# One attention-plus-MoE kernel, one core: another written order ahead of the second chunk, and other places for every temporary

## The chip, the cores and the metric

The kernel runs on one core of one Trainium2 chip. The core has five engines that each work through a list of instructions of their own: TensorE (PE in the profile, its weight loads PEld), VectorE (DVE), ScalarE (ACT), GpSimd (POOL) and SyncE (SP), which here does nothing but issue transfers. The metric is the device time of one execution in microseconds (us).

## The reference

Two steps. The first is attention with 8 batches, 8 heads, 512 local and 32 global positions, head size 64. The local queries see the 32 global keys and the local keys within a window of 32, the global queries see everything:

```
s_ll = where(|i - j| <= 32, scale * q_l k_l^T, -1e9)
a_l  = softmax(concat(scale * q_l k_g^T, s_ll))
out_l = a_l @ concat(v_g, v_l)
out_g = softmax(scale * q_g k_all^T) @ v_all
```

The result is laid out as 4608 tokens of 512 values, and goes through a gated feed-forward layer of width 1536:

```
xn  = x / sqrt(mean(x*x) + 1e-6) * rms_g
g   = xn @ w_gate;  val = xn @ w_val
out = (g * sigmoid(g) * val) @ w_out
```

## The kernel before

**Tiling.** The tokens are worked in nine chunks: eight of 512 local tokens (one batch each) and a last one of the 256 global tokens. Each chunk needs its attention first, then the norm, the first layer (gate and value) and the second layer. Products in the feed-forward layers are made of f16 halves, a high and a low one of every f32 operand, with three matmuls for one. The first chunk's weights come from the inputs; while it and the second chunk run, sums of weights are formed ("folds", function fold at L1487) and stored in DRAM buffers (wa, wb, wd), and the later chunks load those.

**Pieces and their written order.** The whole program is first recorded as small pieces with a name "chunk:step.number"; one piece holds calls of one engine (write, L2076). In the first chunk L loads queries and keys, S makes scores, M takes minima on DVE, E the exponentials on ACT, T and C turn and copy them, V and A are the values, N are the steps of the root, D the factors of the norm, U (on PE) turns and scales an activation block, H and Y split it into a high and a low half, W, m, s, l, k and g prepare weights, I are the 48 pieces of the first layer and O the 24 of the second. "1:P3" is the fourth product of the second chunk, "1:S/0+2" the scores of unit 0 of the chunk after next made beside it, with N and M its minima, "1:n55" steps of the next chunk's norm, "1:w51" a step of a weight fold or load. The table ORDER (L66) lists all 3754 names, and the last loop issues them exactly so:

```
for name in ORDER.split() or list(plan):
    for call in plan.pop(name):
        call()
```

No scheduler moves anything after that: every engine, the transfer queue of SP too, executes its calls in this order and stops at the first that has to wait.

**Places.** Temporaries in the on-chip memory lie in 43 pages of 4 KB and 8 wide pages of 4.5 KB per partition; the table PAGES (L396) gives the place of each temporary in the order in which they are created ("36a" is page 36 from its first quarter on, "w3" wide page 3). The table BANKS (L444) does the same for the 8 accumulator banks of PE. Whoever writes a page or a bank waits until all earlier readers and writers of that part of it are done, engines and transfers alike. SP's transfers go round over eight lanes, and a transfer waits for the one before it on its lane.

**The places that the prediction speaks of.** The fold of the eleventh weight block ends in the piece 1:w51, whose store (L1513 to L1518) reads the original weight page with two transfers and the sums with a third. In the same stretch DVE takes the minima of the scores of 1:S/0+2 (softmax in local_halves, L969), each of which writes a scratch tile of exponentials, and PE makes a small matmul 1:n55.0 of the norm, which writes a bank that these minima read.

Of the kernel before, what the change touches and what calls it, by code (L numbers as in the profile page):

```python
# [20 lines left out]
B, H, SL, SG, D = 8, 8, 512, 32, 64  # L21
# [45 lines left out]
0:L0.0 0:S0.0 0:L2.0 0:S2.0 0:M0.0.2 0:M0.0.0 0:M0.0.1 0:z0.0 0:M0.0.3 0:M0.1.0 0:E0.0.0 0:M2.1.0  # L67
0:M2.1.1 0:M2.1.2 0:M2.1.3 0:M0.1.2 0:L3.0 0:M2.0.2 0:E2.1.0 0:M0.1.1 0:M0.1.3 0:S3.0 0:M3.1.2
0:z1.0 0:z2.0 0:M2.0.1 0:E0.1.0 0:M2.0.3 0:M2.0.0 0:E2.0.0 0:M3.0.3 0:M3.0.2 0:z2.1 0:M3.1.1
0:M3.1.0 0:M3.1.3 0:E3.1.0 0:T0.0.0 0:C0.0.0 0:L1.0 0:M3.0.1 0:M3.0.0 0:E3.0.0 0:W1.0 0:V0.0 0:z2.4  # L70
0:W0.0 0:m1.0 0:T0.1.0 0:T2.0.0 0:W3.0 0:z2.6 0:z2.5 0:l1.0 0:C2.0.0 0:m1.1 0:T2.1.0 0:C0.1.0 0:s1.0
0:l1.1 0:g1.0 0:g1.1 0:q1.0 0:z3.0 0:z4.1 0:T3.1.0 0:z4.0 0:R0.0 0:S1.0 0:M1.0.3 0:M1.0.1 0:M1.0.0
0:M1.0.2 0:V2.0 0:M1.1.1 0:M1.1.0 0:C2.1.0 0:M1.1.2 0:E1.0.0 0:M1.1.3 0:z4.2 0:R2.0 0:z2.2 0:m0.0
0:m0.1 0:s0.0 0:A0.0 0:l0.0 0:m3.0 0:E1.1.0 0:g0.0 0:m3.1 0:k3.0 0:l0.1 0:T1.1.0 0:V1.0 0:T1.0.0
0:p1.0 0:A2.0 0:s3.0 0:X0.0 0:g3.0 0:C1.0.0 0:Q0.0 0:g0.1 0:q0.0 0:T3.0.0 0:C1.1.0 0:g3.1 0:V3.0
0:X2.0 0:z2.3 0:p0.0 0:e0.0 0:e0.1 0:e0.2 0:z5.0 0:C3.0.0 0:Q2.0 0:z6.0 0:W2.0 0:C3.1.0 0:e1.0
0:q3.0 0:R3.0 0:A1.0 0:R1.0 0:Z0.0 0:e1.1 0:z6.1 0:W4.0 0:Z2.0 0:z6.2 0:X1.0 0:A3.0 0:a0.0 0:X3.0
# [2258 lines left out]
```

## Time and profile before

| | |
|---|---|
| times of three runs | 890.65, 890.77, 891.91 us, median 890.77 |
| profiled execution, first to last instruction | 890.5 us, 0.27 us under that median |
| mean granted clock of PE | 0.990 of full speed |
| busy: PE, DVE, ACT, POOL | 864.1, 709.7, 557.9, 277.8 us |
| the transfer queue's share of 16 engines | 70.9% |

In the profile one line of the source, L2095, issues everything, so instructions are told apart by operation, shape and time. "Idle" behind a row is the idle time of the engine ahead of it, and the name behind the arrow is what ended it. The part of the order that the change rearranges ends in this execution at about 168.6 us, when the scores 1:S/0+1 are done.

### The profile page before, as it was taken

What the parts mean: (1) busy time and instruction counts of PE and PEld (TensorE: products, weight loads), DVE (VectorE), ACT (ScalarE), POOL (GpSimd) and SP (SyncE); (2) the same over time, 40 slices, a digit from 0 to 9 for tenths busy, and PEclk for the clock granted to TensorE, in tenths of its full rate; (3) what the DMA queues carried; (4) which work ended last, traced back from release to release, by engine and by line L of the source; (5) the groups of instructions that cost most, each with busy time, mean ns of one, the idle gap of its engine ahead of it and who ended that gap; (6) DMA issues with size and microseconds to landing.
All of it is one profiled execution on the core that took longest, in us unless ns stands there. A gap on an engine that the chain in (4) does not pass through costs nothing.

```text
span 890.5 us, 28310 instructions
## 1 busy us (share of the span) xinstructions
PE 864.1 (97%) x11646; PEld 666.4 (75%) x11646; DVE 709.7 (80%) x1857; ACT 557.9 (63%) x1362; POOL 277.8 (31%) x255
## 2 busy tenths in 40 slices
PE   5599999999999999999999999999999999999998
PEld 4554455545548885588888888888888888888997
DVE  5999999798686776777886899688886798587576
ACT  6999993657344664557473876568575772545343
POOL 0000000024834475414531255123441344124414
PEclk9699999999999999999999999999999999999999
DMA  9995340488974997984697567968796759747671
GB/s 353 407 392 190 96 142 25 141 277 283 374 253 143 288 304 230 312 266 150 218 376 263 172 224 218 339 234 291 254 366 206 253 152 366 262 140 229 229 255 62
DMA packets 102737, 216.79 MB, mean 243 GB/s; under 512 B 8272, under 2 KB 34640, under 8 KB 102608
## 3 DMA queue, kind: packets, MB, share of 16 engines
q1 hardware_dynamic: 102176, 214.66, 70.9%
q8 instruction: 91, 1.49, 0.7%
q10 hardware_dynamic: 432, 0.33, 0.1%
q14 instruction: 38, 0.31, 0.1%
HBM read 187.96 MB, written 27.00 MB: 241 GB/s over the span
## 4 chain that ended last, share of the span: by engine, by line
PE 85%; DMA 3%; DVE 3%; issue 1%; ACT 1%; SPq 1%; POOL 0%; DVEq 0%; POOLq 0%; ACTq 0%
PE bank L2095 85%; DVE page L2095 3%; DMA wide<-wd 1%; DMA page<-in_vb_dram 1%; DMA page<-in_gv_dram 1%; ACT page L2095 1%; DMA wb<-page 1%; SPq L2095 1%; POOL page L2095 0%; DVE wide L2095 0%; DVE xg L2095 0%; DVE ws L2095 0%; DVE sm L2095 0%; DVE hs L2095 0%; DVE pow L2095 0%
## 5 line engine op out<-in xcount | busy, mean ns | idle before, releaser
L2095 PE MATMUL bank<-page,page 128*128 128x256 f16 (+7 forms) x8406 | 726.8, 277 | 16.4 <-ACT page L2095 8.0
L2095 PEld LDWEIGHTS <-page 128*128 128x128 f16 (+1 forms) x5568 | 515.7, 98 | 159.4 <-issue 7.6
L2095 POOL TENSOR_TENSOR page<-page,page 128x512 f16<-128x512 f32 (+5 forms) x163 | 180.0, 1122 | 286.4 <-ACT page L2095 236.1
L2095 DVE TENSOR_TENSOR page<-bank,page 128x512 f32<-128x512 f32 (+1 forms) x179 | 113.9, 649 | 64.2 <-PE bank L2095 37.5
L2095 ACT COPY page<-bank 128x512 f32<-128x512 f32 (+3 forms) x172 | 86.9, 529 | 111.2 <-PE bank L2095 100.0
L2095 ACT CAST page<-page 128x512 f16<-128x512 f32 (+2 forms) x144 | 109.0, 780 | 73.5 <-DVE page L2095 59.9
L2095 ACT ACTIVATE page<-page,sm 128x128 f32<-128x128 f32 x344 | 126.5, 391 | 26.7 <-DVE sm L2095 21.7
L2095 DVE TENSOR_TENSOR page<-page,page 128x256 f32<-128x256 f32 (+4 forms) x145 | 90.5, 636 | 9.0 <-ACT page L2095 7.0
L2095 POOL TENSOR_TENSOR page<-page,sm 128x512 f32<-128x512 f32 x22 | 25.5, 1167 | 208.9 <-DVE sm L2095 201.0
L2095 ACT ACTIVATE page<-page 128x512 f32<-128x512 f32 (+2 forms) x93 | 77.1, 907 | 9.6 <-DVE page L2095 7.2
L2095 DVE CUSTOM_DVE_ANT_0 page<-bank,page 128x128 f32<-128x128 f32 x248 | 60.3, 283 | 19.9 <-PE bank L2095 18.8
L2095 PEld LDWEIGHTS bank<-page,page 64*32 64x32 f32 (+4 forms) x3072 | 55.2, 113 | 24.5 <-issue 11.0
L2095 PE MATMUL bank<-wide,page 32*64 32x96 f32 (+6 forms) x2074 | 63.4, 266 | 1.3 <-DMA page<-in_vb_dram 1.3
L2095 ACT ACTIVATE page<-page,half_inv 128x512 f32<-128x512 f32 (+1 forms) x68 | 44.7, 686 | 23.9 <-DVE page L2095 19.3
L2095 DVE TENSOR_TENSOR page<-page 128x256 f32<-128x256 f32 (+3 forms) x110 | 57.1, 533 | 1.1 <-PE bank L2095 0.2
L2095 PE MATMUL bank<-page,wide 128*128 128x256 f16 (+4 forms) x500 | 56.9, 269 | 0.8 <-DMA wide<-wd 0.8
L2095 DVE SCALAR_TENSOR_TENSOR page<-page,page 128x512 f32<-128x512 f32 (+1 forms) x68 | 46.8, 702 | 12.7 <-ACT page L2095 12.7
L2095 DVE SCALAR_TENSOR_TENSOR page<-page,c_h,page 128x512 f32<-128x512 f32 (+1 forms) x73 | 51.8, 728 | 0.7
L2095 PEld LDWEIGHTS <-wide 128*128 128x128 f16 x450 | 41.6, 98 | 13.9 <-DMA wide<-wd 1.1
L2095 ACT ACTIVATION_READ_ACCUMULATOR page<-page,sm 128x1 f32 x248 | 46.8, 189 | 0.0
L2095 POOL TENSOR_TENSOR page<-wide,page 128x512 f16<-128x512 f32 (+2 forms) x25 | 27.4, 1105 | 45.4 <-ACT page L2095 43.3
L2095 PEld LDWEIGHTS bank<-wide,page 32*64 32x64 f32 (+2 forms) x1936 | 29.5, 129 | 6.8 <-issue 2.7
(156 smaller groups left out, 662.1 us busy)
## 6 DMA issues: line engine op xcount, KB each, us to landing
page<-wd SPq DMA_DIRECT2D x117, 512.0 KB, 6.9
page<-wb SPq DMA_DIRECT2D x36, 512.0 KB, 7.0
page<-in_w_in_dram SPq DMA_DIRECT2D x24, 512.0 KB, 9.3
page<-wa SPq DMA_DIRECT2D x23, 512.0 KB, 6.4
page<-wd SPq DMA_DIRECT2D x42, 256.0 KB, 5.3
page<-in_qkb_dram SPq DMA_DIRECT2D x23, 448.0 KB, 6.1
wide<-in_gkq_dram SPq DMA_DIRECT2D x16, 576.0 KB, 8.1
page<-in_vw_dram SPq DMA_DIRECT2D x16, 512.0 KB, 9.3
```

The lines of the kernel that those rows point to most:

```text
L2095: return lambda *a, **k: write(self.engine, lambda: call(*a, **k))
```

## The change

Three tables change and nothing else: 638 of the 3754 names of ORDER stand at another index, all of them between index 2 and 659; from the piece 0:o0.1 (index 660) on both orders are the same; 1166 of 1198 places in PAGES and 373 of 438 in BANKS differ, in the whole program. The instructions are the same 28310, with the same operands in other places.

```
 ORDER = """
-0:L0.0 0:S0.0 0:L2.0 0:S2.0 0:M0.0.2 0:M0.0.0 0:M0.0.1 0:z0.0 0:M0.0.3 0:M0.1.0 0:E0.0.0 0:M2.1.0
...
+0:L0.0 0:S0.0 0:M0.0.0 0:z0.0 0:M0.0.1 0:M0.0.2 0:M0.0.3 0:E0.0.0 0:M0.1.1 0:M0.1.0 0:z1.0 0:z2.0
...
 PAGES = """
-3a 0c 2a 0c 3c 10a 11a 4c 3c 13a 2a 7a 16a 0a 1a 4c 12a 6a 0a 24a 4a 5a 23a 10c 4a 7a 8a 5a 19a 20a
...
+0a 0c 1a 0c 1a 5a 6a 2a 6a 7a 8a 5a 3a 2a 3a 2a 13a 14a 1c 3a 2c 4a 13a 0c 2c 9a 10a 4a 17a 18a 15a
...
 BANKS = """
-0 1 7 6 1 0 2 3 4 7 6 0 2 5 6 3 4 1 6 5 0 3 4 7 5 2 3 0 1 2 4 5 3 5 7 6 0 6 1 1 5 6 0 1 4 2 7 6 5 3
...
+0 1 1 6 3 2 2 3 4 3 1 2 4 0 5 6 7 4 6 5 0 6 2 3 2 3 0 4 7 0 7 7 3 6 2 6 4 3 6 2 1 6 2 0 0 4 1 5 2 5
```

**First place, PE between the attention and the first layer of the first chunk.** Before, these rows stand there: values of the units (32x64), the four turns of 0:U (128x128), then the scores 0:S4 (32x128).

```order
LDWEIGHTS page_65
MATMUL bank_121<-one_138,page_65 128x1
MATMUL bank_115<-gm,ones 128x2
MATMUL bank_120<-page_82,page_86 32x64 x16
MATMUL bank_120<-page_83,page_86 32x64 x16
MATMUL bank_119<-page_84,page_76 32x64 x16
MATMUL bank_119<-page_77,page_76 32x64 x16
MATMUL bank_115<-page_95,page_80 128x128 x4
MATMUL bank_116<-page_95,page_87 128x128 x4
MATMUL bank_117<-page_95,page_87 128x128 x4
MATMUL bank_114<-page_95,page_80 128x128 x4
MATMUL bank_121<-page_69,page_95 32x128
```

Now the scores 0:S4 (page_85 with page_63) stand between the values and the turns, and the scores 0:S5 (page_73 with page_80) between the second and the third turn:

```order
MATMUL bank_120<-page_80,page_76 32x64 x16
MATMUL bank_120<-page_81,page_76 32x64 x16
MATMUL bank_116<-page_82,page_65 32x64 x16
MATMUL bank_116<-page_70,page_65 32x64 x16
MATMUL bank_116<-page_85,page_63 32x128
...
MATMUL bank_117<-page_63,page_66 128x128 x4
MATMUL bank_114<-page_63,page_66 128x128 x4
MATMUL bank_115<-page_73,page_80 32x128
...
MATMUL bank_121<-page_63,page_64 128x128 x4
MATMUL bank_118<-page_63,page_64 128x128 x4
```

So two score steps of 64 matmuls each have moved ahead of turns that they followed.

**Second place, the store 1:w51 on SP and the minima on DVE.** SP's rows at that store before (wd5 is the DRAM buffer; the number behind the underscore is the memory's own):

```order
DMA page36_99<-in_qkb_dram 128x512 [waits DMAHW4_49]
DMA page19_82<-in_qkb_dram 128x896 [waits DMAHW5_49]
DMA wd5_157<-page0_63 512x1x256 [waits DMAHW6_49]
DMA wd5_157<-page0_63 512x1x256 [waits DMAHW7_49]
DMA wd5_157<-wide5_111 512x1x512 [waits DMAHW0_49]
```

and now:

```order
DMA page37_100<-in_qkb_dram 128x512 [waits DMAHW4_49]
DMA page22_85<-in_qkb_dram 128x896 [waits DMAHW5_49,PE_49]
DMA wd5_157<-page36_99 512x1x256 [waits DMAHW6_49]
DMA wd5_157<-page36_99 512x1x256 [waits DMAHW7_49]
DMA wd5_157<-page5_68 512x1x512 [waits DMAHW0_49,DVE_49]
```

The first two transfers of the store read page 0 before and read page 36 now, on lanes 6 and 7 in both.

DVE's rows shortly behind, at the minima of 1:S/0+2 (the rows that write a page and sm6 from a bank and the mask), before:

```order
TENSOR_REDUCE nt2_32_193<-page27_90 128x16 [waits DVE_49]
TENSOR_TENSOR page31_94<-page31_94 128x256
ISA page36_99,sm6_33_194<-bank1_115,page33_96 128x128 [waits PE_49,Pool_49]
ISA sm6_33_194 128x1
ISA page3_66,sm6_33_194<-bank7_121,page33_96 128x128
...
ISA page41_104,sm6_33_194<-bank3_117,page33_96 128x128 [waits DMAHW6_49,PE_49]
...
TENSOR_SCALAR nt2_32_193<-bank7_121 128x16 [waits PE_49]
```

and now:

```order
TENSOR_REDUCE nt2_32_193<-page8_71 128x16 [waits DVE_49]
TENSOR_TENSOR page27_90<-page27_90 128x256
ISA page14_77,sm6_33_194<-bank1_115,page42_105 128x128 [waits PE_49,Pool_49]
ISA sm6_33_194 128x1
ISA page25_88,sm6_33_194<-bank4_118,page42_105 128x128 [waits DMAHW5_49]
...
ISA page36_99,sm6_33_194<-bank3_117,page42_105 128x128 [waits DMAHW6_49,PE_49]
...
TENSOR_SCALAR nt2_32_193<-bank4_118 128x16 [waits PE_49]
```

The third minimum wrote page 41 before, which an older load on lane 6 had filled, and writes page 36 now, which the store on lane 6 reads. The last row reads what PE's 1:n55.0 has written into the same bank (7 before, 4 now) that the minima around it read.

**Third place, SP's loads ahead of a wait of PE at 309 us.** Before:

```order
DMA page24_87<-wd2_154 128x2x1024 [waits DMAHW0_49]
DMA page41_104<-wd1_153 128x1024 [waits DMAHW1_49,DVE_49]
DMA page37_100<-wd2_154 128x1024 [waits DMAHW2_49,DVE_49,Pool_49]
DMA page2_65<-wd2_154 128x2x1024 [waits DMAHW3_49,DVE_49,PE_49]
DMA page34_97<-wd2_154 128x2x1024 [waits DMAHW4_49,DVE_49]
...
DMA wide7_113<-wd4_156 128x2048 [waits DMAHW3_49]
```

and now:

```order
DMA page30_93<-wd2_154 128x2x1024 [waits DMAHW0_49]
DMA page33_96<-wd1_153 128x1024
DMA wide4_110<-wd2_154 128x1024
DMA wide7_113<-wd2_154 128x2x1024 [waits DMAHW3_49]
DMA wide1_107<-wd2_154 128x2x1024 [waits DMAHW4_49,DMAHW5_49,DVE_49,Activation_49]
...
DMA page37_100<-wd4_156 128x2048 [waits DMAHW3_49,PE_49]
```

Three of these loads waited for DVE to release their page, and wait for no engine now.

## Rows read from the trace of the kernel before

**Rows 1.** The page's part 4: the chain that ended last, by line.

```profile
PE bank L2095 85%; DVE page L2095 3%; DMA wide<-wd 1%; DMA page<-in_vb_dram 1%; DMA page<-in_gv_dram 1%; ACT page L2095 1%; DMA wb<-page 1%; SPq L2095 1%; POOL page L2095 0%; DVE wide L2095 0%; DVE xg L2095 0%; DVE ws L2095 0%; DVE sm L2095 0%; DVE hs L2095 0%; DVE pow L2095 0%
```

**Rows 2.** Who PE waited for from 47 us on: total, times, longest.

```profile
PE bank L2095 <- DMA page<-in_vb_dram: 1.3, 1, 1.3
PE bank L2095 <- DMA wide<-wd: 0.8, 1, 0.8
```

**Rows 3.** Timeline of PE, start: start, length, operation, count, idle before.

```profile
30.45 2.18 PE L2095 MATMUL bank<-page,page 128*32 128x64 f32 x128
40.06 6.47 PE L2095 MATMUL bank<-page,page 128*128 128x128 f32 x96 [7.44 <-ACT page L2095]
```

**Rows 4.** Windows: length, busy PE, PEld, DVE, ACT, POOL; PE's clock; DMA.

```profile
24.00:30.00 6.00, 6.00 (x94) 4.88 (x94) 5.32 (x10) 5.97 (x14) 0.00 (x0) 0.52 1.03 410
34.00:38.00 4.00, 0.00 (x0) 0.00 (x0) 3.54 (x14) 4.00 (x7) 0.00 (x0) 0.82 1.04 407
38.00:42.00 4.00, 1.94 (x9) 1.97 (x10) 3.93 (x12) 4.00 (x6) 0.00 (x0) 0.50 1.03 410
42.00:46.00 4.00, 4.00 (x70) 3.88 (x73) 4.00 (x7) 2.75 (x6) 0.00 (x0) 0.83 1.03 404
0.00:47.00 47.00, 28.98 (x680) 23.26 (x681) 36.09 (x152) 38.57 (x108) 0.20 (x4) 0.82 0.99 382
```

**Rows 5.** Groups of instructions, 0 to 166 us, PE: busy us, mean ns, idle before.

```profile
L2095 PE MATMUL bank<-page,page 64*32 64x128 f32 x512 | 11.6, 318 | 7.1 <-DMA page<-in_qk_dram 6.4 <-DVE page L2095 0.7
```

**Rows 6.** The same for DVE, 0 to 47 us: the minima.

```profile
L2095 DVE CUSTOM_DVE_ANT_0 page<-bank,page 128x128 f32<-128x128 f32 x32 | 7.1, 287 | 8.4 <-PE bank L2095 8.4
```

**Rows 7.** Timeline of DVE, 243 to 246 us: the minima of 1:S/0+2.

```profile
243.63 0.28 DVE L2095 CUSTOM_DVE_ANT_0 page<-bank,page 128x128 f32<-128x128 f32 x1
...
244.06 0.28 DVE L2095 CUSTOM_DVE_ANT_0 page<-bank,page 128x128 f32<-128x128 f32 x1
...
245.11 0.08 DVE L2095 DVE_READ_ACCUMULATOR2_ANT sm<- 128x1 f32 x1
```

**Rows 8.** Timeline of PE's weight loads, 243 to 247 us.

```profile
243.10 1.61 PEld L2095 LDWEIGHTS <-page 128*128 128x128 f16 x8
245.24 0.30 PEld L2095 LDWEIGHTS bank<-nt,same 128*128 128x128 f32 x2 [0.53 <-DVE sm L2095]
```

**Rows 9.** Timeline of SP, 239.6 to 242 us: the store 1:w51.

```profile
239.90 1.85 SPq L2095 DMA_DIRECT2D wd<-page  x2
```

**Rows 10.** The tile wd, 239.85 to 239.95 us: that store's first transfer.

```profile
DMA to landing us min/median/max: 9.2/9.2/9.2
```

**Rows 11.** Waits of SP, 206 to 218 us.

```profile
SPq L2095 <- DVE page L2095: 9.6, 1, 9.6
```

**Rows 12.** Windows: DMA's share and GB/s are the last two columns.

```profile
217.00:257.00 40.00, 39.96 (x528) 20.31 (x527) 32.41 (x91) 17.98 (x54) 21.20 (x17) 1.00 1.01 348
280.00:288.00 8.00, 8.00 (x238) 6.93 (x217) 4.22 (x9) 3.34 (x7) 1.42 (x2) 1.00 0.12 38
```

**Rows 13.** Transfer issues of the whole program: count, KB each, median us to landing.

```profile
out_dram<-page SPq DMA_DIRECT2D x14, 256.0 KB, 3.6
```

**Rows 14.** Timeline of PE, two later waits.

```profile
309.52 1.48 PE L2095 MATMUL bank<-page,wide 128*128 128x256 f16 x12 [0.81 <-DMA wide<-wd]
...
433.65 2.35 PE L2095 MATMUL bank<-wide,page 32*64 32x256 f32 x158 [1.34 <-DMA page<-in_vb_dram]
```

**Rows 15.** Waits of SP, 276 to 289.95 us.

```profile
SPq L2095 <- DVE page L2095: 14.4, 3, 8.7
```

**Rows 16.** The chain, 295 to 312 us: start, length, what.

```profile
301.45 8.02 DMA wide<-wd
```

**Rows 17.** Timeline of SP, 414 to 428 us.

```profile
423.21 0.32 SPq L2095 DMA_DIRECT2D page<-wa  x1
425.03 0.37 SPq L2095 DMA_DIRECT2D page<-wd  x1
425.45 0.93 SPq L2095 DMA_DIRECT2D page<-in_vb_dram  x2
```

More of the change, by code (lines that the diff above doesn't have):

```diff
@@ L72 @@
[L72 to L77, printed above, removed]
@@ L273 @@
[L273 to L275 removed]
+0:L0.0 0:S0.0 0:M0.0.0 0:z0.0 0:M0.0.1 0:M0.0.2 0:M0.0.3 0:E0.0.0 0:M0.1.1 0:M0.1.0 0:z1.0 0:z2.0
+0:M0.1.3 0:L2.0 0:S2.0 0:M2.0.2 0:M2.1.3 0:M0.1.2 0:E0.1.0 0:T0.0.0 0:L3.0 0:S3.0 0:L1.0 0:S1.0
+0:M2.1.0 0:M2.1.2 0:M3.0.0 0:z2.1 0:z2.4 0:z2.6 0:M2.1.1 0:E2.1.0 0:z2.5 0:z3.0 0:T2.1.0 0:M3.0.3
@@ new lines @@
+2:w4.0 1:Y/2+1.0 1:P45.0 1:Y/2+1.1 1:Y/2+1.2 2:w9.0 1:Y/2+1.3 1:R45.0 2:L/2+1.0 1:P48.0 1:R46.0
+1:R47.0 1:P49.0 1:R45.1 1:P60.0 1:n53.0 1:R48.0 1:R49.0 1:w51.0 1:n53.1 1:S/0+2.0 2:w63.0 2:w20.2
+1:N1/0+2.0 1:N0/0+2.0 1:N3/0+2.0 1:N0/0+2.1 1:M0/0+2.0 1:M1/0+2.0 1:M0/0+2.1 2:w2.0 1:w47.0
+1:M3/0+2.1 1:P67.0 1:w35.0 1:P68.0 1:n55.0 1:R33.1 1:n55.1 1:n55.2 1:n55.3 1:n55.4 1:P61.0
+1:E0/0+2.0 1:w54.0 1:N3/0+2.1 1:w54.1 1:N2/0+2.0 1:M2/0+2.1 1:n55.5 2:w20.3 2:w20.4 1:F0/0+2.0
+1:M3/0+2.0 1:E3/0+2.0 1:M2/0+2.0 1:E2/0+2.0 1:n55.6 1:n55.7 1:n55.8 1:n55.9 1:N2/0+2.1 1:F2/0+2.0
@@ new lines @@
+1:n55.10 1:n55.11 1:n55.12 1:n55.13 1:n57.1 1:n57.0 1:n56.0 1:n56.1 1:n58.0 1:P50.0 1:n59.0 1:w54.3
+2:w2.1 2:w11.1 2:w15.0 1:P54.0 2:w2.2 2:w2.3 1:P55.0 1:D2/0+2.0 1:n59.1 1:P51.0 1:P69.0 1:D2/0+2.1
+1:P56.0 2:w13.0 2:w4.1 1:P70.0 1:P52.0 1:P71.0 1:D0/0+2.0 1:D0/0+2.1 1:P62.0 1:P53.0 1:T2/0+2.0
+1:n64.1 1:P63.0 1:n65.0 2:w20.0 1:P57.0 1:P58.0 1:P59.0 1:R71.0 1:T0/0+2.0 1:w54.2 1:P64.0 2:w5.0
+1:n58.1 1:n63.2 1:F3/0+2.0 1:D3/0+2.0 1:w54.4 1:n59.2 1:R59.0 1:w56.0 1:n60.0 1:n61.0 2:P1.0 1:n61.1
+1:w57.0 1:w59.0 2:P0.0 2:R1.0 2:R0.0 1:P65.0 1:D3/0+2.1 2:R2.1 1:n63.0 1:n62.1 1:N1/0+2.1 1:n63.1
@@ new lines @@
+2:M3/0+2.0 2:N2/0+2.1 2:F0/0+2.0 2:D0/0+2.0 2:w47.2 2:M1/0+2.0 2:E1/0+2.0 2:w65.0 3:w60.0 2:P53.0
+2:P60.0 2:P54.0 2:P47.0 2:P55.0 2:n47.13 2:n49.1 2:R47.0 2:N1/0+2.0 2:F1/0+2.0 2:M3/0+2.1 2:P56.0
+2:P57.0 2:n50.0 2:n50.1 2:n49.0 2:n51.0 2:n52.0 2:P61.0 2:P62.0 3:w24.0 2:R53.0 2:w56.0 2:E3/0+2.0
+2:F3/0+2.0 2:D3/0+2.0 2:n52.1 2:D0/0+2.1 2:R53.1 2:w47.3 2:D1/0+2.0 2:R47.1 2:n53.0 2:N2/0+2.0
+2:n55.1 2:n56.1 3:GS/1+1.0 2:n56.2 2:n54.0 2:P63.0 3:w53.0 2:n51.1 2:E2/0+2.0 2:n54.1 2:V/0+2.0
+2:n56.0 2:D3/0+2.1 3:GM/1+1.0 3:GM/1+1.1 2:n58.1 2:n55.0 2:T0/0+2.0 2:P58.0 2:P64.0 2:P59.0
@@ new lines @@
+3:D0/0+2.1 6:w38.0 5:w6.0 3:n47.0 3:R56.0 3:O36.0 3:O37.0 3:O38.0 3:O39.0 3:O40.0 3:T0/0+2.0
+3:D1/0+2.1 3:T3/0+2.0 3:T1/0+2.0 3:w57.0 4:w40.0 3:n48.1 3:O41.0 3:D2/0+2.1 3:R53.0 5:w10.0 3:n47.1
+3:n48.0 3:n49.0 3:T2/0+2.0 3:A/0+2.0 3:n49.2 3:n49.1 4:w34.0 3:n51.1 3:n53.2 4:L/2+1.0 3:R59.0
+3:n50.0 4:P1.0 4:w1.0 4:w4.0 4:R1.0 3:n54.1 3:n51.0 3:n52.0 4:P2.0 3:R62.0 4:P7.0 4:P0.0 3:n52.1
+4:R2.0 4:R0.0 3:n55.0 4:P5.0 3:B/0+2.0 4:Y/0+1.0 4:R1.1 3:n53.0 4:w13.0 4:w22.0 3:n53.1 4:R5.0
+3:n54.0 4:P3.0 3:X/0+2.1 3:n55.1 4:P8.0 3:X/0+2.0 4:R8.0 4:Y/0+1.1 3:n56.0 4:R7.0 4:P4.0 4:R8.1
```

475 lines of the change are left out of this document (227 added, 248 removed), and 18 rows, old and new, of the table BANKS.

## The prediction

> **What bounds the kernel now.** I read the chain that ended last first: 85% of it is PE's own work [rows 1], so the kernel is as long as PE's list plus PE's waits. The table of PE's waits from 47 us on shows how few there are: the longest is 1.3 us for a load of values and the next 0.8 us for a load of weights [rows 2]. Before 47 us PE is busy for only 28.98 us of 47 [rows 4]; the largest hole is the 7.44 us in front of the turns 0:U, in which ACT and DVE finish the first attention [rows 3]. A change of order and places that keeps every instruction can therefore do three things: shorten or lengthen the hole before 47 us, remove the two late waits, and add a wait where a new place is still in use.
>
> **Term 1, the rearranged stage (0 to 168.6 us): 0.** The pieces are the same up to its end, so each engine has the same work there, and only its waits can change. Two score steps run ahead of turns that they followed. One such step costs 11.6 / 8 = 1.45 us of PE, with 512 matmuls in the row and 64 in a step [rows 5]. One of them, 0:S4, falls into the 7.44 us hole and is then gone from the time behind it: a gain of up to 1.45 us. Against it, the eight minima of each step come earlier on DVE, at 7.1 / 32 = 0.22 us each [rows 6], and DVE, with 36.09 us of 47 busy and hardly a gap close to the turns, in 34 to 38 and 38 to 42, 3.54 and 3.93 of 4 us [rows 4], feeds those turns. Seven minima ahead of the last turns would be 1.5 us. When I lay the new lists of PE, ACT and DVE beside each other with the durations of the trace, the turns start within 0.2 us of before, the first layer about 0.5 us later, and the score step that has gone ahead makes up for it before the end of the stage. I take 0, with -1.45 and +1.5 as ends.
>
> **Term 2, a new wait of DVE for a store: +5.1.** In the second place that the order shows, the store 1:w51 now reads page 36, and the third minimum of 1:S/0+2, close behind, writes page 36. It has to wait until the store's first transfer has landed. In the trace that transfer is issued at 239.90 [rows 9] and takes 9.2 us to land [rows 10], so to 249.1; the minimum started at 244.06 [rows 7]. DVE would stand for 249.1 - 244.06 = 5.0 us. PE is not covered: its small matmul 1:n55.0 already waited 0.53 us for DVE and started at 245.24 [rows 8], right behind the read that ends at 245.11 + 0.08 = 245.19 [rows 7]. That read stands in the same distance behind the waiting minimum in both orders. So PE's start moves from 245.24 to about 245.24 + 5.05 = 250.3, and what is queued behind it on PE, the rest of the second chunk's products, moves along. Nothing gives it back, as PE has no later wait of over 0.7 us except the two of [rows 14].
>
> Is the landing the same with the new places? It follows from how the transfers are backed up: DMA is full from 217 to 257 us (share 1.01 [rows 12]), and SP there issues as lanes come free. That backlog begins when a hold of 9.6 us on a page of DVE ends [rows 11], and this hold stands in the new order as well, on the same fold piece. Issue and landing should come at the same times within some tenths.
>
> Bounds: below, a store that finds the queue empty. The nearest row is 256 KB stores of the output at 3.6 us [rows 13]; then it would land at 243.5, ahead of the minimum, and the term is 0. Above, the third transfer of the same store, or the next store, landing later only matters to writers further behind. I take 5.1, by the row of this very transfer.
>
> [...]
>
> **Term 3, PE's clock after that wait: +1.7.** PE would stand from 243.10 + 1.61 = 244.7 (its last weight load) to 250.3, 5.6 us. [...] Ends: 0 if the clock stays, and 6 x (1 - 0.52) = 2.9 by the other slow stretch, 24 to 30 us [rows 4]. I take 1.7.
>
> [...]
>
> **Term 4, the two late waits: -1.7.** The load that ends PE's 0.81 us at 309.52 [rows 14] is issued at 301.45 and lands 8.02 us later [rows 16]. SP had been held by pages of DVE for 14.4 us between 276 and 290 [rows 15], and DMA was almost idle, 0.12, from 280 to 288 [rows 12]; then all loads came at once. In the third place shown, three of these loads wait for no engine any more. They go out into the idle stretch, so I count the whole 0.8 us. For the wait of 1.34 us at 433.65 [rows 14], SP's issues come at 423.21, 425.03 and 425.45 [rows 17]; the load at 425.03 waited for a page that PE read until then. With its new page it can go at once after 423.21 + 0.32 = 423.5, and the two loads behind it are then bound by readers about 0.9 us earlier than now. I count 0.9. Ends: 0 and -2.2, the whole of both.
>
> Elsewhere, from 168.6 us on, I walked through every wait that a new place makes, with the times of the trace: others are late by under 1 us on engines that are idle there, and cost nothing while ACT and POOL have their gaps.
>
> **The sum.** Profiled span 890.5 + 0 + 5.1 + 1.7 - 1.7 = 895.6; the median of the runs is 0.27 above that span, so 895.9 us.
>
> **Rivals.**
> - The clock stays full after the wait. [...] 895.9 - 1.7 = 894.2.
> - The store lands in time. One mechanism: SP, held less for pages, issues the transfers ahead of 239.9 earlier, and the store finds a shorter queue. The point from which it decides is a landing at 244.0, 5 us sooner; from there on terms 2 and 3 are gone, and 890.77 - 1.7 = 889.1 stays, faster. For it: the order shows fewer engine waits on SP. Against it: the hold of 9.6 us ahead of that stretch stays, and with DMA at 1.01 an earlier issue only waits longer. [...] A landing between 245 and 247 would leave about 1 to 3 us of the wait, eaten by term 4: no change.
> - The stage itself gains or loses more than its ends, since 18 us of PE's idle lie there (47 - 28.98). If the turns start 2 us sooner, PE arrives sooner at 1:n55.0, but the landing, tied to the backlog, moves with DVE's hold; 894. If two units' exponentials come late for the turns, 898.
>
> **Chances.** Forecast (wait and slow clock) 0.50; wait at full clock 0.20; store in time, or nearly, 0.20, of which half faster; stage off by 2 us or more with the wait in place 0.10, slower all the same in nearly all of it. Less than 0.2% (1.8 us) can't be told from no change here. Faster 0.11, within it 0.12, slower 0.77. The range: up to 898.5 (clock as in 24 to 30 us, +1.2, and the stage's +1.5), down to 890.0, which leaves out the store in time. The forecast's own range is 893.5 to 898.5.
>
> **What would show it.** In the profile after: DVE idle for about 5 us at 244 to 249 with a DMA store as releaser; PE idle some 5.5 us just ahead of the two small matmuls of 1:n55.0, and a clock near 0.5 for 2 to 4 us behind it; no wait for wide<-wd or page<-in_vb_dram of more than 0.5 us on PE; PE's first layer starting between 46.5 and 48.5. If DVE shows no such wait, term 2 and with it the forecast is wrong; if the span up to 168.6 differs by over 1.5 us, term 1 is.

## The result and the profile after

The changed kernel takes 904.65 us (median of 4 runs, 903.41 to 905.39) against 891.34 us for the kernel before on the same chip: 1.0142 times as long, 95% interval 1.0121 to 1.0163. It is slower, as forecast, but by 13.3 us where 5.1 were forecast, and the time lies outside the range, 6.2 us above its upper end.

The forecast wait is there. DVE's timeline after: the third minimum of 1:S/0+2 stands 5.11 us for the store, where in [rows 7] it starts 0.43 us behind the first, at 244.06.

```profile
249.35 0.28 DVE L2095 CUSTOM_DVE_ANT_0 page<-bank,page 128x128 f32<-128x128 f32 x1
249.56 0.08 DVE L2095 DVE_READ_ACCUMULATOR2_ANT sm<- 128x1 f32 x1
254.75 0.29 DVE L2095 CUSTOM_DVE_ANT_0 page<-bank,page 128x128 f32<-128x128 f32 x1 [5.11 <-DMA wd<-page]
```

The store on SP's timeline, issued at 245.94 where [rows 9] has 239.90:

```profile
245.94 4.08 SPq L2095 DMA_DIRECT2D wd<-page  x3
```

The tile wd from 245.8 to 246.1 us, that store's first transfer: it lands after 8.7 us, where [rows 10] has 9.2.

```profile
DMA to landing us min/median/max: 8.7/8.7/8.7
```

PE's timeline at the same place: its last work ahead of the wait ends at 250.70, and the small matmuls of 1:n55.0 start at 255.94, after 5.24 us of waiting. Before, their weight load had waited 0.53 us [rows 8].

```profile
247.94 2.76 PE L2095 MATMUL bank<-page,page 128*128 128x512 f16 x12
255.94 0.61 PE L2095 MATMUL bank<-nt,same 128*128 128x16 f32 x2 [5.24 <-DVE sm L2095]
256.39 5.92 PE L2095 MATMUL bank<-page,page 128*128 128x512 f16 x19
```

The windows behind it (length; busy PE, PEld, DVE, ACT, POOL; PE's clock; DMA): the clock is 0.53 for 4 us and full after that.

```profile
250.00:256.00 6.00, 0.76 (x5) 0.16 (x2) 1.25 (x11) 0.45 (x3) 0.23 (x1) 0.75 1.07 383
256.00:260.00 4.00, 4.00 (x12) 1.68 (x13) 3.70 (x18) 1.45 (x8) 0.00 (x0) 0.53 1.10 361
260.00:264.00 4.00, 4.00 (x20) 1.86 (x19) 3.76 (x17) 2.62 (x13) 0.00 (x0) 1.00 0.84 255
```

PE's waits from 47 us on (total, times, longest). The loads wide<-wd and page<-in_vb_dram of [rows 2] are not in the list any more. The wait that the store makes leads it (PE waits for DVE, which waits for the store), and "issue", time in which PE waits for nothing that the profile shows, is new.

```profile
PE bank L2095 <- DVE sm L2095: 5.2, 1, 5.2
PE bank L2095 <- issue: 2.5, 3, 1.3
PE bank L2095 <- DVE page L2095: 2.0, 5, 1.1
PE bank L2095 <- DVE gsm L2095: 1.0, 1, 1.0
```

The largest loss that was not forecast begins ahead of 47 us. PE's timeline of the start, against [rows 3]: the four products of the first attention stand close together from 26.38 on, two of them broken by an "issue" gap, the turns start at 43.10 instead of 40.06, and the first product of the first layer at 51.66 instead of 47.11. The score step at 36.90 (two rows, with another gap) is the one that was to fill the hole.

```profile
14.91 0.88 PE L2095 MATMUL bank<-page,page 64*32 64x128 f32 x41 [2.35 <-issue]
...
26.38 3.64 PE L2095 MATMUL bank<-page,page 128*32 128x64 f32 x128 [1.70 <-ACT page L2095]
...
33.31 2.79 PE L2095 MATMUL bank<-page,page 128*32 128x64 f32 x96 [0.91 <-issue]
36.90 1.10 PE L2095 MATMUL bank<-page,page 64*32 64x128 f32 x31 [0.80 <-DVE page L2095]
39.08 0.70 PE L2095 MATMUL bank<-page,page 64*32 64x128 f32 x33 [1.08 <-issue]
43.10 7.41 PE L2095 MATMUL bank<-page,page 128*128 128x128 f32 x96 [3.31 <-DVE page L2095]
51.66 2.09 PE L2095 MATMUL bank<-page,page 128*128 128x512 f16 x8 [1.15 <-DVE page L2095]
```

The first layer in the kernel before:

```profile
47.11 10.57 PE L2095 MATMUL bank<-page,page 128*128 128x512 f16 x48
```

Ahead of its first layer PE idles 19.5 us in after and 17.7 in before. So 1.8 of the 4.55 us are more idle time; the rest is work, the score steps that now stand ahead of it and slower matmuls.

Windows of the same stretch: the clock is at its half level while those products run, and 0.76 on the mean to 47 us, where [rows 4] has 0.82.

```profile
26.00:30.00 4.00, 3.62 (x129) 3.45 (x129) 3.30 (x8) 3.84 (x8) 0.00 (x0) 0.50 1.03 410
30.00:36.00 6.00, 5.09 (x151) 4.77 (x148) 4.26 (x13) 5.12 (x7) 0.00 (x0) 0.50 1.03 402
...
0.00:47.00 47.00, 28.55 (x658) 23.50 (x666) 33.30 (x158) 35.52 (x101) 0.20 (x4) 0.76 0.97 367
```

The start of the same piece on PE in both traces gives the account of the loss:

| piece on PE | before | after | later by |
|---|---|---|---|
| first turn 0:U0 | 40.06 | 43.10 | 3.04 |
| 1:P10, second chunk, the rearranged stage is over | 175.40 | 179.10 | 3.70 |
| 1:P22, behind a wait of DVE at 199.87 | 205.99 | 211.48 | 5.49 |
| 1:n55.0, the wait | 245.24 | 255.94 | 10.70 |
| 1:P54, clock full again | 248.07 | 260.64 | 12.57 |
| 2:P28, first late wait gone | 309.52 | 321.20 | 11.68 |
| 3:P40, second one gone | 437.91 | 448.53 | 10.62 |
| end of the span | 890.5 | 902.6 | 12.1 |

From 1:P10 to 1:P22 nothing was rearranged, and still 1.79 us are lost. It is a second wait for a store, at one of the new places: DVE stands 1.78 us ahead of 199.87, and PE waits for DVE behind it, 1.01 us ahead of 203.30 and the rest in smaller steps up to 1:P22.

```profile
199.87 1.23 DVE L2095 TENSOR_TENSOR page<-page 128x1024 f32<-128x1024 f16 x1 [1.78 <-DMA wd<-page]
```

```profile
203.30 4.04 PE L2095 MATMUL bank<-page,page 128*128 128x512 f16 x18 [1.01 <-DVE gsm L2095]
```

From 3:P40 to the end another 1.5 us are lost; the two longest pieces are "issue" gaps of PE, 0.42 us at 451.27 and 0.83 at 653.60.

### The profile page after: what moved, and what is told of

The parts are those of the page before. It is cut to its first block, busy times and chain, and to the rows that moved or that the text cites. A ratio compares the mean times of both kernels' runs of the same rounds, so it can differ in the third digit from the quotient of the medians.

```text
span 902.6 us, 28331 instructions
## 1 busy us (share of the span) xinstructions
PE 868.5 (96%) x11646; PEld 669.6 (74%) x11646; DVE 709.8 (79%) x1857; ACT 559.5 (62%) x1362; POOL 278.9 (31%) x255
## 4 chain that ended last, share of the span: by engine, by line
PE 52%; DVE 2%; issue 1%; DMA 0%; POOL 0%; ACT 0%; SPq 0%; DVEq 0%; POOLq 0%
PE bank L2095 52%; DVE page L2095 2%; DMA wa<-page 0%; POOL page L2095 0%; ACT page L2095 0%; DVE wide L2095 0%; SPq L2095 0%; POOL wide L2095 0%; DVEq L2095 0%; POOLq L2095 0%; ACT wide L2095 0%
## 5 line engine op out<-in xcount | busy, mean ns | idle before, releaser
L2095 PE MATMUL bank<-page,page 128*128 128x256 f16 (+7 forms) x7290 | 686.4, 284 | 22.3 <-issue 6.9
L2095 PEld LDWEIGHTS <-page 128*128 128x128 f16 (+1 forms) x5247 | 482.7, 98 | 158.7 <-issue 12.9
L2095 DVE TENSOR_TENSOR page<-bank,page 128x512 f32<-128x512 f32 (+1 forms) x165 | 103.3, 640 | 61.5 <-PE bank L2095 40.4
L2095 PE MATMUL bank<-page,wide 128*128 128x256 f16 (+4 forms) x1172 | 117.7, 279 | 0.2 <-POOL wide L2095 0.2
L2095 PEld LDWEIGHTS <-wide 128*128 128x128 f16 x771 | 74.9, 98 | 21.5 <-POOL wide L2095 0.5
L2095 DVE TENSOR_TENSOR page<-page,page 128x256 f32<-128x256 f32 (+4 forms) x135 | 81.0, 608 | 7.1 <-ACT page L2095 5.5
L2095 PE MATMUL bank<-wide,page 32*64 32x96 f32 (+9 forms) x2261 | 75.8, 257 | 0.0
L2095 ACT ACTIVATE page<-page 128x512 f32<-128x512 f32 (+2 forms) x83 | 69.4, 896 | 9.9 <-DVE page L2095 5.9
L2095 DVE SCALAR_TENSOR_TENSOR page<-page,c_h,page 128x512 f32<-128x512 f32 (+1 forms) x61 | 42.9, 721 | 0.5
L2095 DVE STREAM_TRANSPOSE wide<-page 128x512 f32<-128x512 f32 x45 | 30.4, 694 | 4.1 <-POOL page L2095 4.0
```

The lines of the kernel that those rows point to most:

```text
L2095: return lambda *a, **k: write(self.engine, lambda: call(*a, **k))
```

## The experiments

Times are medians; the ratio is to runs of the kernel before on the same chip (891.3 to 892.3 us), with its 95% interval. Tiles are named as the program names them; a page number with a letter is a place.

**One half of the change at a time.** e1 has the new order with the old late places, e2 the old order with the new late places. The early places could not be kept: 45 and 42 tiles had to be put elsewhere, which is an edit of its own.

```
e1: ORDER of after   PAGES, BANKS: late ones of before, 45 early tiles moved
e2: ORDER of before  PAGES, BANKS: late ones of after, 42 early tiles moved
```

> The new order with the old places from 168 us on (the tiles of the first stage keep the new places, 45 of them and 16 banks moved to free ones). Theory of parts: the rearranged stage alone costs about 4 us and the old late waits of 0.8 and 1.3 us are back, no wait of 5 us at the minima: 894 to 896.5, about 895.5. Rival (places are everything, the late stage is only what full pages made of it): within 1 us of the kernel before, 890 to 892.

> The old order with the new places for all that lives beyond 168 us (early tiles keep the old places, 42 of them and 8 banks moved to free ones). Theory of parts: the wait at the minima (5.1) and the slow clock behind it (1.9), less the two late waits (1.9): 895 to 897, and PE reaches the product in front of the wait at the time of before. Rival (the wait grew out of the late stage): 889 to 891, no wait of over 2 us at the minima.

e1: 910.12 us, ratio 1.0209 (1.0178 to 1.0239), far over its range. PE is 18.9 us late at 1:P10, with the order that made 3.70 in after, so the moved early places stall the stage by themselves and the time says little; but from 168 us on it has no wait of DVE for that store. e2: 902.61 us, 1.0117 (1.0102 to 1.0132), 5.6 us over its range: PE is already 3.5 us late ahead of 1:n55.0, where it was expected to be on time. But with the old order, PE waits 5.5 us there. So the store's wait belongs to the places, not to the order of the pieces.

**The store's wait by itself.** e3 takes the one tile of the waiting minimum off the store's page in the kernel after; e4 puts it onto a page that this store reads in the kernel before (two other tiles make room).

```diff
 e3, after:          e4, before:
-e611 at 36a        -e611 at its old place
+e611 at W7a        +e611 at 0a   (gx0 to W0, h2_2 to W5)
```

> The changed kernel with one tile of 1198 in another place: the scratch tile of the third minimum of 1:S/0+2 goes from page 36 to wide page 7, which nothing near it uses. Theory of parts: 5.2 us of wait and 1.9 us of slow clock go, about 897.5 (896.5 to 898.5). Rival (something else is late behind the wait, DVE's own list or the next store): under 3 us gained, 901.5 or more.

> The kernel before with the same one tile put onto the page that the store 1:w51 reads (page 0 there; two other small tiles step aside). Theory of parts: one place of 1198 costs 7 us, 897 to 898.5, of which 5 us are PE's wait and about 1.9 us the half clock behind it. Rival (PE is covered, or the clock stays): 891 to 896.

e4: 899.78 us, 1.0084 (1.0068 to 1.0101), 1.3 us over its range. One tile's place makes the whole wait, 5.74 us on DVE:

```profile
249.96 0.29 DVE L2095 CUSTOM_DVE_ANT_0 page<-bank,page 128x128 f32<-128x128 f32 x1 [5.74 <-DMA wd<-page]
```

and the half clock behind it, in e4's windows:

```profile
244.00:250.00 6.00, 1.27 (x6) 0.39 (x4) 0.26 (x4) 0.00 (x0) 0.81 (x1) 0.87 1.08 376
250.00:254.00 4.00, 2.85 (x8) 1.31 (x9) 3.74 (x21) 1.85 (x9) 0.00 (x0) 0.50 1.07 355
254.00:258.00 4.00, 4.00 (x17) 1.71 (x16) 3.76 (x22) 2.17 (x11) 0.00 (x0) 0.84 0.61 215
```

In e4 PE is late by 5.91 us at 1:n55.0, by 7.90 behind the half clock, by 6.83 at 2:P28 and by 5.79 at 3:P40. Both late waits of [rows 14] are gone there too, although every late load has its old place. The loads do move with the delay: SP issues wide<-wd at 308.49 and page<-in_vb_dram at 432.29, 7.04 and 6.84 us later than before ([rows 16], [rows 17]). They end up in time by little: PE was 7.65 us late ahead of the first, which lands in 7.8 us instead of 8.0, and the second lands within 6.3 us of its issue instead of 7.55. Why they land sooner is not shown.

e3: 901.47 us, 1.0108 (1.0093 to 1.0123), only 3.2 us less than after, where 7 were expected: what its rival named is what happened. The wait at 1:n55.0 is gone (0.45 us), but DVE now comes in time for two further stores and stands there:

```profile
254.45 1.23 DVE L2095 TENSOR_TENSOR page<-page 128x1024 f32<-128x1024 f16 x1 [4.48 <-DMA wd<-page]
260.62 0.71 DVE L2095 STREAM_TRANSPOSE wide<-nt 128x512 f32<-128x512 f32 x1 [1.25 <-DMA wd<-wide]
```

PE meets that 20 us later:

```profile
274.81 3.17 PE L2095 MATMUL bank<-page,page 128*128 128x256 f16 x24 [3.67 <-DVE page L2095]
280.84 4.42 PE L2095 MATMUL bank<-page,page 128*128 128x256 f16 x39 [1.46 <-DVE page L2095]
```

**All the tiles that wait for stores.** e5 is after with four tiles moved; e7 has the new stage with the old places renumbered as a whole behind it (28 tiles moved).

```diff
 e5, after:
-e611 36a, wq11 5a, y2 W1a, e601 36c
+e611 W7a, wq11 4a, y2 W7c, e601 30c
```

> The changed kernel with four tiles moved: the third minimum's tile of 1:S/0+2 (page 36 to page W7), and the three tiles behind it that wait for stores (page 5 to 4, page W1 to W7, page 36 to page 30). Theory: the rest of the loss is the rearranged stage, +3.7 us at 1:P10 and some +1 to +2 behind it by a wait for DVE's sums at 1:P20, less the two late waits that the new places take away: 893.7 to 895.5 us, no wait of PE of over 1 us between 230 and 300 us, full clock there. Rival 1, the stage's loss is only borrowed and PE catches up at the first products: 889 to 890.5. Rival 2, each store wait taken away uncovers another: over 898, with a wait of PE of over 3 us between 230 and 300 us.

> The changed kernel's order and places up to 168 us and the old places (renumbered as a whole, 28 tiles moved) behind it. Theory: the rearranged stage alone costs 3.7 us at 1:P10, whatever places follow; the store wait is absent; the two late waits of PE shrink by the delay as they did when a delay of 6 us was made ahead of them, by up to 2: 892.5 to 895 us. Rival, the stage's rearrangement is neutral and the loss of 3.7 us comes of the new places behind it: 890 to 891.5.

e5: 896.42 us, 1.0064 (1.0046 to 1.0082), 0.9 us over its range. Between 230 and 300 us PE keeps no wait of 1 us, and the median is 8.2 us under that of after. What is left is the stage, +3.20 at 1:P10, and the wait at 199.87, which the four moves did not touch: DVE stands 1.70 us there and PE is +4.90 at 1:P22. e7: 901.99 us, 1.0124 (1.0107 to 1.0141), 7 us over its range: the renumbering gave the transpose that waits in e3 another store (5.86 us on DVE, 3.27 on PE at 275.60). It shows the stage's part with other late places, +3.83 at 1:P10, and the same +3.83 at 1:P22, since DVE does not wait at this point there.

In all the traces with the new order what PE loses from 1:P10 to 1:P22 is, within 0.02 us, what DVE waits for that store: 1.78 in after, 1.70 in e5, 1.76 in e9 and e13, 1.79 in e15, 0.3 to 0.4 in e8, e12 and e14, nothing in e1, e3 and e7. No trace with the old late places has the wait. So these 1.8 us come with the new late places and not with the rearranged stage. e2 and e3 have those places too and do not have the wait; what decides it there, and what moving this one tile would bring, was not tried.

**The late waits by themselves.** e6 is the kernel before with the tiles of the loads that held SP at free places.

```diff
-wt2_13 41a, wt2_23 37a, wt2_21 2a, wt2_22 34a, wt5_01 2a, v90 4a
+wt2_13 W5a, wt2_23 W0a, wt2_21 W4a, wt2_22 W3a, wt5_01 W6a, v90 W2a
 (room: et101 w6 to w7, u_2 W6a to 2a, et121 w6 to w0)
```

> The kernel before with other places for nine tiles (six that loads write between 274 and 290 us and at 425 us, which held the loads' queue until DVE or PE had read the old contents, and three that make room). Order of instructions unchanged. Theory of the prediction's term 4: the loads go out early into an idle DMA and the two late waits of PE (0.81 us at 309.5 and 1.34 us at 433.7) go: 888.7 to 890.0 us, 0.9 to 2.1 under the kernel before. Rival: PE only arrives earlier at later things (as it arrives later at them, and loses the waits, when it is delayed by 6 us), and a later wait gives it all back: 890.5 to 891.5, with a new or longer wait of PE behind 309 or 433 us.

892.16 us, 1.0006 (0.9997 to 1.0015): no gain. The late waits did go; PE's timeline of e6 shows 0.20 us at 309.96, and none at 433. But in this execution the second pair of attention products ran at half clock, in 3.44 us instead of the 2.18 of [rows 3], with the same code. The turns came 1.48 us later; 0.77 of that was there before the pair, and 1.26 came with the clock, of which the hole ahead of the turns took some back:

```profile
31.22 3.44 PE L2095 MATMUL bank<-page,page 128*32 128x64 f32 x128
...
309.96 1.48 PE L2095 MATMUL bank<-page,wide 128*128 128x256 f16 x12 [0.20 <-DMA wide<-wd]
```

The window 30 to 34 us of the kernel before, and then of e6:

```profile
30.00:34.00 4.00, 2.62 (x139) 2.29 (x135) 3.60 (x15) 4.00 (x8) 0.00 (x0) 1.00 1.03 405
```

```profile
30.00:34.00 4.00, 4.00 (x118) 3.97 (x121) 2.96 (x13) 4.00 (x8) 0.00 (x0) 0.50 1.03 408
```

e6's turns are 1.48 us late and its span ends 0.4 early (890.1), so PE regains 1.9 us, most of it at the two late waits (+1.31 at 1:P54, -0.60 at 3:P40). But old late places give most of that back too: in e4 2.1 of a delay ahead of them, and in e10 below, which has the same half-clock pair, +1.09 at 1:P54 becomes -0.44 at 3:P40. By these two traces e6's places bring some 0.4 us when the pair ran at half clock. The time of the pair differs from one trace of the old order to the next: 2.18, 2.02 and 2.03 us in before, e4 and e2 (clock 0.98 to 1.00 from 30 to 34 us), 3.44, 3.40 and 3.64 in e6, e10 and e11 (clock 0.50). How often it is slow in the executions that were not profiled is not shown: the mean granted clock is 0.990 in all 11 runs of e6, but also in the profiled execution of the kernel before, whose pair ran at full clock.

**What delays the stage.** e8 is e5 with the first value product early; e9 is e5 with the score step between the turns put behind them (and one tile moved, 17a to W5a); e12 has both.

```diff
 e8:  ... 0:T1.1.0 +0:V0.0 +0:A0.0 ...   0:C0.1.0 +0:C0.0.0 ...  -(their later places)
 e9:  -0:U0.1.0 0:S5.0 0:U0.3.0     +... 0:I1.00.0 0:I0.00.0 0:S5.0
      -0:M5.1.2 0:M5.0.1 ahead of 0:Y0   +behind 0:q2.0
```

> As the changed kernel with four tiles moved, and in the stage the copy 0:C0.0.0 back ahead of the query pieces, and the values 0:V0.0 and the first attention's product 0:A0.0 back to just behind 0:T1.1.0 (where the kernel before had them). Theory: the turns 0:U0 start 3 us late because the four attention products run in a row at half clock from 26.4 us on; with the first value early the turns start 1.5 to 2.6 us sooner than in the changed kernel (at 40.5 to 41.6), 1:P10 starts 1 to 2 us sooner, and the time is 1 to 2 us under that of the kernel with the four tiles moved alone. Rival: DVE's list (more minima and masks ahead of the turns) sets the start of the turns; they start within 0.5 us of 43.1 and the time is the same within 0.5 us.

> As the changed kernel with the four tiles moved, and in the stage the sixth score step 0:S5.0 (which stands between the turns 0:U0.1 and 0:U0.3) behind the first two products of the first layer, its first two minima behind 0:q2.0. Theory: a score step between the turns, at half clock and with its minima ahead of the sums 0:Y0 on DVE, holds the first layer back: it starts 1.3 to 2 us sooner than the 51.7 us of the changed kernel, 1:P10 by 0.6 to 1.5 us sooner, the time 0.6 to 1.5 us under that of the kernel with the four tiles moved (896.4): 894.9 to 895.8 us. Rival: only the late first values count; the first layer starts within 0.4 us of 51.7 and the time is 896.0 to 896.8 us.

> As the changed kernel with the four tiles moved, with both edits of the stage: first values early, and the sixth score step behind the first layer's first products. Theory: the two causes add up, 0.6 to 1.5 us under the kernel with the values early alone (894.8): 893.2 to 894.2 us; 1:P10 within 0.7 us of the kernel before. Rival: both shorten the same hole, and the time stays at 894.5 to 895.2 us.

e8: 894.77 us, 1.0039 (1.0025 to 1.0052); 1:P10 is late by 0.89 instead of 3.20. The products come apart and run faster, at a clock of 0.91 in 24 to 30 us where after has 0.50 in 26 to 30; in PE's timeline of e8 the first two take 1.25 and 1.10 us, where after needed 3.64 for both:

```profile
24.77 1.25 PE L2095 MATMUL bank<-page,page 128*32 128x64 f32 x64
26.44 1.10 PE L2095 MATMUL bank<-page,page 128*32 128x64 f32 x64 [0.42 <-ACT page L2095]
...
31.80 2.69 PE L2095 MATMUL bank<-page,page 128*32 128x64 f32 x95 [1.13 <-issue]
...
41.47 7.05 PE L2095 MATMUL bank<-page,page 128*128 128x128 f32 x96 [2.77 <-DVE page L2095]
```

The medians differ by 1.65 us, as expected, though the two intervals overlap a little. Of the 2.31 us that PE gains at 1:P10, 1.68 are there at 80 us; the rest comes with an "issue" gap, 1.13 us at 148.57 in e5, where e8 has a wait of 0.51. e9: 896.17 us, 1.0042 (1.0027 to 1.0057), and e12: 894.97 us, 1.0038 (1.0028 to 1.0049). Between e12 and e8 the score step between the turns makes no difference. e9 against e5 is unclear: the medians agree and the ratios do not, and in its trace the first layer starts at 48.72 instead of 51.17 and 1:P10 0.81 us sooner.

**The score step in the hole.** e10 is the kernel before with 0:S4.0 on PE moved ahead of the turns (one bank changes); e11 also has the sums 0:Y0.1 and 0:Y0.0 ahead of three weight pieces on DVE, 0:e0.3 a little ahead, and e6's places.

```diff
 e10: 0:Z3.0 +0:S4.0 ... 0:U0.2.0 ... -0:S4.0
 e11: 0:Y0.1.0 0:Y0.0.0 +0:g4.0 +0:g4.1 +0:m7.1 +0:q4.0   (from ahead of 0:Y0.1.0)
```

> The kernel before with one part of the change alone: the fifth score step 0:S4.0 on PE moved from behind the turns 0:U0 into the idle 7.4 us ahead of them (its eight minima stay where they were; two banks change). Theory of the prediction's term 1: 1.15 to 1.45 us of PE leave the time behind the turns, and the turns start at a higher clock, since PE was busy in 37 to 39 us: first layer at 45.9 to 46.8 instead of 47.1, time 889.5 to 890.8 us. Rival: the first layer waits for the chain of ACT and DVE (0:H0, 0:Y0) behind the turns, not for the score step, so the step was hidden already, and the late waits of PE give back the rest: 891.2 to 892.0 us.

> The kernel before with the score step 0:S4.0 ahead of the turns, three weight pieces (0:g4.0, 0:g4.1, 0:m7.1, with 0:q4.0) moved behind the sums 0:Y0.1 and 0:Y0.0 on DVE, 0:e0.3 a little ahead, and the nine tiles of the loads that held the queue at other places. Theory: the first layer starts at 45.0 to 46.0 us instead of 47.1, and the gain reaches the end because the two late waits that would shrink or grow against it are gone: 888.0 to 890.0 us. Rival: gains ahead of the late loads and without the late waits still do not reach the end, because a later wait of the same kind takes them: 891.0 to 892.0 us.

e10: 891.42 us, 0.9995 (0.9986 to 1.0004); e11: 892.42 us, 1.0009 (1.0001 to 1.0018). The step went into the hole, and nothing came of it that the times show. In PE's timeline of e10 the first layer waits 0.93 us for DVE:

```profile
37.34 1.82 PE L2095 MATMUL bank<-page,page 64*32 64x128 f32 x64 [2.77 <-DMA page<-in_qk_dram]
41.45 5.22 PE L2095 MATMUL bank<-page,page 128*128 128x128 f32 x32 [2.29 <-DVE page L2095]
...
48.12 8.12 PE L2095 MATMUL bank<-page,page 128*128 128x512 f16 x36 [0.93 <-DVE page L2095]
```

This execution had the half-clock pair too, so e6 is the trace to hold it against: there the first layer starts at 48.44. The step in the hole moves it by 0.32 us, and 1:P10 by 0.20. The theory's higher clock at the turns did not come: it is 0.50 in 38 to 42 and 0.70 in 42 to 46 us, where [rows 4] has 0.50 and 0.83.

**The rest of the stage.** e13 is e8 with five minima of the fifth step behind 0:Y0.1, e14 is e8 with 0:S1.0 behind two transposes, e15 has both.

```diff
 e13: -0:M4.1.1 0:M4.0.0 0:M4.1.2 0:M4.0.3 0:M4.0.1   +behind 0:Y0.1.0   (the last from between the turns)
 e14: 0:L1.0 -0:S1.0 ... 0:T3.1.0 ... 0:T3.0.0 +0:S1.0
```

> As the kernel with the first values early (and the four tiles moved), and the four minima of the fifth score step that stand on DVE ahead of 0:D0 behind the sum 0:Y0.1. Theory: these four, 4 x 0.21 us, stand on the path to the turns, as DVE has hardly a gap there; the turns start 0.6 to 0.9 us sooner than with the values early alone and the time is 0.4 to 0.9 us under its 894.8: 893.9 to 894.4 us. Rival: the turns are late by the queue of ACT or by PE, not by the minima; the time stays within 0.4 us of 894.8.

> As the kernel with the first values early (and the four tiles moved), and the score step 0:S1.0, inside which PE stands 1.7 to 2.4 us at 12.8 us for its instructions (a 16 KB instruction transfer lands 1.5 us ahead of its restart), behind the transposes 0:T3.1.0 and 0:T3.0.0. Theory: the pause delays DVE's 0:z4.0 and with it the first attention; with other work in its place the pause falls into a wait or goes, DVE's idle 1.3 us at 15 us shrinks, 0:A3.0 starts 0.5 to 1.3 us sooner and the time is 0.4 to 1.3 us under 894.8. Rival: the pause comes with the place in the program, not with the work there, and holds whatever stands there: no gain, 894.4 to 896.0 us.

> Both edits, the fifth step's minima behind the first sum and the score step 0:S1.0 later, beside the first values early and the four tiles moved. Theory: the rest of the stage's loss against the kernel before (3.1 us in the medians) is made of these two and of the half clock; 892.6 to 893.8 us. Rival: the rest is spread over many small places of the new order, and these two edits together bring under 0.4 us: 894.4 us or more.

e13: 896.07 us, 1.0042 (1.0029 to 1.0055). e14: 897.90, 1.0071 (1.0048 to 1.0093), its runs spread over 8 us. e15: 899.71, 1.0085 (1.0067 to 1.0103). No theory of the three comes true. In e13 the turns did start 1.18 us sooner than in e8 (0.6 to 0.9 expected), but PE stood again behind them:

```profile
40.29 7.76 PE L2095 MATMUL bank<-page,page 128*128 128x128 f32 x96 [1.24 <-DVE page L2095]
49.06 2.10 PE L2095 MATMUL bank<-page,page 128*128 128x512 f16 x8 [1.00 <-DMA page<-in_w_in_dram]
52.39 1.04 PE L2095 MATMUL bank<-page,page 128*128 128x512 f16 x4 [1.23 <-DVE page L2095]
```

In e14 the "issue" gap of 2 us at 13 us is gone. Twelve transposes that took 2.20 us in after take 4.63, and the step starts at 17.70, the first product at 27.24 (24.77 in e8):

```profile
13.14 4.63 PE L2095 MATMUL bank<-ident,page 128*128 128x128 f32 x12
17.70 1.96 PE L2095 MATMUL bank<-page,page 64*32 64x128 f32 x64
...
27.24 2.98 PE L2095 MATMUL bank<-page,page 128*32 128x64 f32 x105
```

The transposes wait for ACT: each takes a block of exponentials, and ACT makes one every 0.39 us in the same stretch of after, from 13.42 to 17.28; the twelve take 0.39 us each here. Who the weight loads waited for from 13 to 17.7 us, in e14:

```profile
PEld bank L2095 <- ACT page L2095: 2.6, 11, 0.3
```

So e14 put the score step behind ACT's exponentials, and does not test what the gap costs.

## Why the prediction was right and wrong

The profiled spans give the account, term by term, in us:

| term | forecast | measured |
|---|---|---|
| 1, the rearranged stage, to 1:P10 | 0 | +3.70 |
| elsewhere: the wait at 199.87, to 1:P22 | 0 | +1.79 |
| 2, the wait at 1:n55.0 | +5.1 | +5.21 |
| 3, the clock behind it, to 1:P54 | +1.7 | +1.87 |
| 4, the two late waits, to 3:P40 | -1.7 | -1.95 |
| behind 3:P40 | 0 | +1.5 |
| sum | +5.1 | +12.1 |

**Term 1 failed.** It said 0, with +1.5 as the upper end, and that the turns start within 0.2 us of before. They started 3.04 us late, and the stage cost 3.70 us at 1:P10 (3.20 in e5, 2.83 in e3 and 3.83 in e7). The working laid the new lists beside each other with durations of the trace, as if a duration went with the instruction. It goes with the clock as well: the pair of products that took 2.18 us in the trace shown took 3.40 to 3.64 in three other executions with the same order up to there, at 1.00 and 0.50 from 30 to 34 us. The new order, which makes the first value late and puts all four products close together, ran them at 0.50. e8 gives that order and its clock a size together: 1.65 us in the medians, 2.31 at 1:P10. One other piece can be seen and was not in the working, the "issue" gap of 1.26 us at 149.08 in after. The other error is the gain side: a score step placed in the hole was to be worth up to 1.45 us. In e10 it moves the first layer by 0.32 us and the time by nothing; the first layer waits 0.93 us for DVE there. The 0.89 us by which e8 is late at 1:P10 stays without a shown cause. e8 is 3.1 us over the kernel before in the medians (1.0039), but this is not all the stage: in its trace PE is 0.48 us early at 3:P40 and 1.28 late at the end, with "issue" gaps between, the longest 0.48 us at 440.23. Neither the step between the turns (e12), nor the fifth minima (e13), nor the place of the second score step (e14) brought any of the 3.1 back.

**"Elsewhere" failed too.** The walk through the waits behind 168.6 us put the others at nothing, as under 1 us on engines that are idle there. DVE's wait at 199.87 was 1.78 us and went through to PE in full.

**Term 2 was right**: +5.1 forecast, 5.11 us on DVE and 5.24 on PE measured, made by one tile's place (e4, e3). That the number fits so well is partly luck: issue and landing were to stay where they were, but the store was issued 6.04 us later and DVE was ready for the third minimum 5.58 later (249.64). Without a delay ahead, in e4, DVE waits 5.74. In after the store's first transfer lands 8.7 us after its issue, with DMA full (1.07 in 250 to 256). What the term missed did not show in the total: two more stores were hidden behind this one (e3). The working put them aside, as transfers whose landing "only matters to writers further behind"; without the first wait those writers stand 4.48 and 1.25 us.

**Term 3 was right**: +1.7 forecast; from 1:n55.0 to 1:P54 PE falls back by a further 1.87, at a clock of 0.53 from 256 to 260 us, and in e4 by 1.99, at 0.50 from 250 to 254. No run shows the 1.7 itself, an estimate of the author's; the runs show 1.87 and 1.99 in its place. In both traces the hole costs more than its length: the delays of 5.21 us (without what was lost ahead of it) and 5.91 at 1:n55.0 grow to 7.08 and 7.90.

**Term 4 was right in its sign and size; its reason is not shown.** The two waits are gone and PE regains 1.95 us from 1:P54 to 3:P40 (1.7 forecast). But e4 regains 2.1 with the old places, so a delay ahead shrinks these waits as well, though the loads move along with it. e6, with free places for these loads alone, brings no gain in the medians.

**Behind 3:P40** the sum had nothing; 1.5 us were lost there, most of it around the "issue" gaps at 451.27 and 653.60.

**The base** was low. The sum set the time 0.27 us above the span, the median of three runs against the span of one execution; in every later execution the time is 1.7 to 2.2 us above its span (904.75 and 902.6 in after). Of the 8.8 us by which the forecast missed, 7.0 lie in the terms and 1.8 here.

Of the rivals, the third (a stage off by 2 us or more, with the wait in place) came closest; it had a chance of 0.10 and reached 898. By the prediction's own signs, a first layer outside 46.5 to 48.5 us, the profile refutes term 1 and none of the other numbered terms; the wait at 199.87 had no sign of its own.

## What to carry to other kernels

A new place for a tile is priced by the last transfer that still reads it (5.74 us of DVE for one tile in e4), and every store in a full queue has to be looked at, also those that another wait now hides (4.48 and 1.25 us in e3): take the first wait away, and walk through the list again. A short wait can count in full where the engine that stands feeds PE, as at 199.87: 1.78 us on DVE, 1.79 on PE. In a start-up stage where PE is idle two fifths of the time (28.98 us busy of 47 here), the profiled durations of PE are one draw of its clock: the same pair of products took 2.02 to 2.18 us at 0.98 to 1.00 and 3.40 to 3.64 at 0.50. An edit there needs bounds from both clock levels. A wait far from the edit can swallow part of a delay made ahead of it, 2.1 us of 7.9 in e4. So read the start of the same piece in both traces, stage by stage, and do not judge a stage by the end of the run alone.

No version tried beats the kernel before: the nearest, e10, is at 0.9995 with an interval that holds 1.

## What was not expected of the hardware

PE stops inside a piece without a wait that the profile shows, for 2.35 us ahead of 14.91 in after. There one 16 KB transfer of the instruction queue moves in the window 12.3 to 15 us (packets, MB, share), while the load queue is full; it lands at 13.42, and PE, with 41 matmuls of its score step to go, restarts at 14.91.

```profile
q1 hardware_dynamic: 301, 1.10, 100.8%
q8 instruction: 1, 0.02, 2.2%
```

Five more such gaps (33.31, 39.08, 149.08, 451.27 and 653.60 us) end 1.3 to 1.6 us after a 16 KB transfer of that queue lands. Which engine's instructions a transfer carries is not shown, so that PE stands there for its instructions, as e14's expectation has it too, is the author's guess from these times. The kernel before shows no such gap on PE. Its transfers of that queue land at 13.17, 21.88, 28.00 and 35.15 us; 1.3 to 1.6 us behind the second and the fourth PE stands for ACT anyway. Why none shows behind the other two, and how to hide the gap, was not settled.
